# Grouped-query attention over a cache: K transposed as 4-byte words, and most of wo loaded behind V

## The chip, the cores and the metric

The kernel runs on one core of a Trainium2 chip. The metric is the device time in microseconds of one execution. Before the change the median of 11 runs is 196.08 us (195.16 to 197.15).

In the text PE is TensorE (matmuls and transposes), DVE is VectorE, ACT is ScalarE, POOL is GpSimd, and SP is the engine whose queue issues all DMA transfers here. SBUF is the on-chip memory, PSUM the memory into which PE writes.

## The reference

The kernel computes one attention block with keys and values from a cache, for 8 batches of 4 query tokens, all in bf16:

```python
B, Sq, D = 8, 4, 512
Hq, Hkv, Sk, Dh = 32, 8, 2048, 128
q = (x @ wq).reshape(B, Sq, Hq, Dh).transpose(0, 2, 1, 3)
k = jnp.repeat(k_cache, Hq // Hkv, axis=1)
v = jnp.repeat(v_cache, Hq // Hkv, axis=1)
p = softmax(einsum("bhqd,bhkd->bhqk", q, k) * Dh ** -0.5)
o = einsum("bhqk,bhkd->bhqd", p, v)
return o.transpose(0, 2, 1, 3).reshape(B, Sq, Hq * Dh) @ wo
```

k_cache and v_cache are 32 MB each, wq and wo 4 MB each. So some 72 MB are read once, and each key meets only the 16 query rows (4 heads of 4 tokens) of its group.

## The kernel before, in words

**Tiles.** Work is cut into 32 units: a pair p of K/V heads (4 of them, outer) and a batch b (8, inner). A unit's K block is one tile `k_sb` of 128 partitions: partitions 0 to 63 hold the first head of the pair, 64 to 127 the second, and each partition holds 32 successive keys of 128 numbers, 8 KB. A "chunk" is the 128 keys with one index c of these 32. One transfer of 1 MB loads it (L87); V is laid out in the same way (L97). There are 7 K buffers and 6 V buffers.

**Steps.** A unit has two steps of 16 chunks each. The loop at the end of the listing runs over the steps, and the order in which Python calls the helpers is the order on each engine: it is written out by hand. In one turn it transposes for step + 7, scores for step + 6, and does the values of the step itself.

- `transpose_part` (L169) turns 8 chunks of K, one PE transpose each, into one PSUM tile `kp` (3 buffers). The tile is copied to SBUF as `kt` (6 buffers) by DVE, and every fourth time by ACT (L172, L174).
- `scores` (L185) runs 16 matmuls per step. The weights are a transposed chunk, 128 by 128; the moving operand is q of both heads, 32 columns. So each key is scored with the queries of both heads, and the exponentials (L191, ACT) read the half that belongs to its own head, written to `probs`. The other half of `probs` stays zero.
- `values` (L205) runs 16 matmuls per step, V chunks as weights and 32 columns of `probs` moving.
- `norms` (L219) sums `probs` with two matmuls of 512 columns, and DVE reduces and inverts (L227, L231). `finish` (L236) scales into `oT_all`.

**The projection.** For each p, `to_tokens` (L248) and `to_wo_rows` (L263) rearrange the 8 heads of the pair into the rows in which wo was loaded, and `project` (L272) runs 8 matmuls of 512 columns, one for each eighth r of wo's block p. For p 0 and 1 this stands behind steps 59 and 61. For p 2 and 3 it follows the last step, with `to_tokens(3)` and `to_wo_rows(3)` between the parts of p 2. At the end DVE and ACT each convert half of the output and SP stores it.

**Transfers.** SP issues x, wq, and then the list `loads`: K of unit u, V of unit u - 3, and at its end wo blocks 0 and 1 between the last V blocks, so V 29, wo 0, V 30, wo 1, V 31. `load_ready` issues from the list as far as buffers allow. Behind step 51, wo block 2, and block 3 in three parts, are issued (L104). The schedule keeps eight transfers in flight.

**Start.** wq is needed whole before q can be made: 128 matmuls of 32 columns (L149), after which ACT scales q into `qT_all` (L156). The K transposes come after them on PE.

Of the kernel before, what the change touches and what calls it, by code (L numbers as in the profile page):

```python
# [8 lines left out]
BF16 = mybir.dt.bfloat16  # L9
FP32 = mybir.dt.float32  # L10
# [4 lines left out]
def kernel(  # L15
# [9 lines left out]
    nc = tc.nc  # L25

    B, Sq, D = x.shape
    _, Hkv, Sk, Dh = k_cache.shape
    HqDh = wq.shape[1]
# [3 lines left out]
    R = D // 128  # L33
    G2 = Hkv // 2
    C = 2 * Sk // 128
    NQ = 2 * rep * Sq
    HC = C // 2
    HP = 2 * rep
    scale = float(Dh) ** -0.5
    NU = G2 * B  # L40
    NH = 2 * NU
# [4 lines left out]
    WR = HP  # L46
# [4 lines left out]
    assert Dh == 128 and C == 32 and NQ == 32 and G2 == 4  # L51

    const = ctx.enter_context(tc.tile_pool(name="const", bufs=1))
    kpool = ctx.enter_context(tc.tile_pool(name="kpool", bufs=KB))
    vpool = ctx.enter_context(tc.tile_pool(name="vpool", bufs=VB))
    ktpool = ctx.enter_context(tc.tile_pool(name="ktpool", bufs=6))
    small = ctx.enter_context(tc.tile_pool(name="small", bufs=2))
    psum_k = ctx.enter_context(tc.tile_pool(name="psum_k", bufs=3, space=bass.MemoryType.PSUM))
    psum_s = ctx.enter_context(tc.tile_pool(name="psum_s", bufs=2, space=bass.MemoryType.PSUM))
# [4 lines left out]
    order = ctx.enter_context(tc.manual_schedule())  # L64

    x_sb = const.tile([T, D], BF16, name="x_sb")
    wq_sb = const.tile([128, R, HqDh], BF16, name="wq_sb")
    xT_sb = const.tile([128, R, T], BF16, name="xT_sb")
    qT_all = const.tile([128, G2, B, HP, Sq], BF16, name="qT_all")
    oT_all = const.tile([128, Hq, B, Sq], BF16, name="oT_all")  # L70
    wo_sb = const.tile([128, G2, WR, D], BF16, name="wo_sb")
    out_sb = const.tile([T, D], BF16, name="out_sb")
    oP = [const.tile([128, WR, T], BF16, name=f"oP{p}") for p in range(G2)]
    ident = const.tile([128, 128], BF16, name="ident")
# [4 lines left out]
    ks = [None] * NU  # L79
# [22 lines left out]
    def load_wo(p, r0, n):  # L102
        rows = wo[p * HP * 128 : (p + 1) * HP * 128, :].rearrange("(q r) j -> q r j", r=WR)
        nc.sync.dma_start(wo_sb[:, p, r0 : r0 + n, :], rows[:, r0 : r0 + n, :])  # L104
# [3 lines left out]
    loads = []  # L108
    for u in range(NU + KA):
        if u < NU:  # L110
            loads.append(("k", u))
        if u >= KA - 1 and u - KA + 1 < NU:
            loads.append(("v", u - KA + 1))
        if u in (NU, NU + 1):
            loads.append(("wo", u - NU))
    loads.reverse()

    def load_ready(nk, nv):
# [12 lines left out]
    load_ready(0, 0)  # L131

    make_identity(nc, ident[:])
    nc.vector.memset(ones[:, :], 1.0)
    for t in probs:
        nc.vector.memset(t[:, :, :], 0.0)
# [7 lines left out]
    for p in range(G2):  # L144
        psq = psum_s.tile([128, HP, T], FP32, tag="s", name="psq")
        for h in range(HP):
            hh = p * HP + h
            for r in range(R):
                nc.tensor.matmul(  # L149
                    psq[:, h, :],  # L150
                    lhsT=wq_sb[:, r, hh * 128 : (hh + 1) * 128],
                    rhs=xT_sb[:, r, :],
                    start=(r == 0),
                    stop=(r == R - 1),
                )
        nc.scalar.mul(  # L156
            out=qT_all[:, p, :, :, :],
            in_=psq[:, :, :].rearrange("d h (b s) -> d b h s", b=B),
            mul=scale,
        )  # L160

    kt = {}

    def transpose_part(i, part):
        u, hf = divmod(i, 2)
        c0 = hf * HC + part * (HC // 2)
        kp = psum_k.tile([128, HC // 2, 128], BF16, tag="k", name="kp")
        for c in range(HC // 2):
            nc.tensor.transpose(kp[:, c, :], ks[u][:, c0 + c, :], ident[:, :])  # L169
        k_t = ktpool.tile([128, HC // 2, 128], BF16, tag="kt", name="kt")  # L170
        if part == 1 and hf == 1:
            nc.scalar.copy(out=k_t[:, :, :], in_=kp[:, :, :])  # L172
        else:
            nc.vector.tensor_copy(out=k_t[:, :, :], in_=kp[:, :, :])  # L174
        kt[(i, part)] = k_t

    def scores(i):
        u, hf = divmod(i, 2)
        p, b = units[u]
        pr = probs[u % len(probs)]  # L180
        s_ps = psum_s.tile([128, HC, NQ], FP32, tag="s", name="s_ps")
        q2 = qT_all[:, p, b, :, :].rearrange("d h s -> d (h s)")
        for c in range(HC):
            k_t = kt[(i, c // (HC // 2))]
            nc.tensor.matmul(  # L185
                s_ps[:, c, :], lhsT=k_t[:, c % (HC // 2), :], rhs=q2, start=True, stop=True
            )
        for g in range(2):
            rows = slice(g * 64, (g + 1) * 64)
            cols = slice(g * NQ // 2, (g + 1) * NQ // 2)  # L190
            nc.scalar.activation(  # L191
                out=pr[rows, hf * HC : (hf + 1) * HC, cols], in_=s_ps[rows, :, cols], func=EXP
            )
# [3 lines left out]
    def values(i):  # L197
        u, hf = divmod(i, 2)
        p, b = units[u]
        pr = probs[u % len(probs)]  # L200
        if hf == 0:
            o_ps[u] = psum_o.tile([128, NQ], FP32, tag="o", name="o_ps")
        for c in range(HC):
            cc = hf * HC + c
            nc.tensor.matmul(  # L205
                o_ps[u][:, :],
                lhsT=vs[u][:, cc, :],
                rhs=pr[:, cc, :],
                start=(cc == 0),
                stop=(cc == C - 1),  # L210
            )
# [3 lines left out]
    def norms(u):  # L215
        pr = probs[u % len(probs)]
        l_ps = psum_l.tile([128, LC, NQ], FP32, tag="l", name="l_ps")
        for c in range(0, C, LC):
            nc.tensor.matmul(  # L219
                l_ps[:, :, :],  # L220
                lhsT=ones[:, :],
                rhs=pr[:, c : c + LC, :],
                start=(c == 0),
                stop=(c + LC == C),
            )
        l_sb = small.tile([128, NQ], FP32, tag="l_sb", name="l_sb")
        nc.vector.tensor_reduce(  # L227
            out=l_sb[:, :], in_=l_ps[:, :, :].rearrange("d c q -> d q c"), axis=AX, op=ADD
        )
        r_sb = small.tile([128, NQ], FP32, tag="r_sb", name="r_sb")  # L230
        nc.vector.reciprocal(r_sb[:, :], l_sb[:, :])  # L231
        r_sbs[u] = r_sb

    def finish(u):
        p, b = units[u]
        nc.vector.tensor_tensor(  # L236
            out=oT_all[:, p * HP : (p + 1) * HP, b, :],
            in0=o_ps[u][:, :].rearrange("d (h s) -> d h s", h=HP),
            in1=r_sbs[u][:, :].rearrange("d (h s) -> d h s", h=HP),
            op=mybir.AluOpType.mult,  # L240
        )
# [18 lines left out]
    def to_wo_rows(p):  # L260
        perm = psum_l.tile([128, WR, T], BF16, tag="l", name="perm")
        for r in range(WR):
            nc.tensor.transpose(  # L263
                perm[:, r, :],
                nats[p][:, :, :].rearrange("t q r -> t r q")[:, r, :],
                ident[:T, :T],
            )
        nc.vector.tensor_copy(out=oP[p][:, :, :], in_=perm[:, :, :])

    def project(p, r0, n):  # L270
        for r in range(r0, r0 + n):
            nc.tensor.matmul(  # L272
                out_ps[:, :],
                lhsT=oP[p][:, r, :],
                rhs=wo_sb[:, p, r, :],
                start=(p == 0 and r == 0),
                stop=(p == G2 - 1 and r == WR - 1),
            )

    for step in range(-L - 1, NH):  # L280
        i, j = step + L + 1, step + L
        if i < NH:
            transpose_part(i, 0)
        if 0 <= j < NH:
            scores(j)
        if i < NH:
            transpose_part(i, 1)
        u, hf = divmod(step, 2)
        if step >= 0:
            p, b = units[u]  # L290
            if hf == 1:
                norms(u)
            values(step)
            if hf == 1:
                finish(u)
            elif p > 0 and b == 1:
                to_tokens(p - 1)
            elif p > 0 and b == 2:
                to_wo_rows(p - 1)
        load_ready(min((i + 1) // 2, NU), max((step + 1) // 2, 0))  # L300
        if step == NH - 1 - 2 * VB:
            assert not loads
            load_wo(2, 0, WR)
            load_wo(3, 0, 4)
            load_wo(3, 4, 2)
            load_wo(3, 6, 2)
        if step == NH - 5:
            out_ps = psum_s.tile([T, D], FP32, tag="s", name="out_ps")
            project(0, 0, WR)
        elif step == NH - 3:  # L310
            project(1, 0, WR)

    to_tokens(3)
    project(2, 0, 4)
    to_wo_rows(3)
    project(2, 4, 4)
    project(3, 0, 4)
    project(3, 4, 2)
    project(3, 6, 2)
# [33 lines left out]
```

## Time and profile before

One profiled execution took 196.83 us. The page counts a span of 195.1 us from the first to the last instruction; 1.73 us lie around it.

| What | Value |
|---|---|
| Median of 11 runs | 196.08 us |
| Profiled execution, its span | 196.83 us, 195.1 us |
| PE busy | 150.3 us, 77% |
| DVE busy | 107.7 us, 55% |
| ACT busy | 84.0 us, 43% |
| DMA | 76.03 MB, 390 GB/s on average |
| K transposes, L169 | 1024, 222 ns each |
| Scores, L185 | 1024, 177 ns each |
| Copies of kt on DVE, on ACT | 96 of 688 ns, 32 of 1012 ns |

How to read it: matmuls run in a pipeline, so the 222 ns of one transpose is its latency; how far apart two of them start is what counts, and the timeline tells that. "busy tenths" gives for each engine 40 equal slices of the span, here 4.88 us each, with the busy share in tenths. PEclk is the share of its full clock that TensorE was granted. The chain that ended last goes back from the last instruction and names at each step what released it. In the timeline a line gives the start, the length, the engine and line of the source, output and inputs, and in brackets how long the engine sat idle before and what ended that.

### The profile page before, as it was taken

Reading aid. Unit: us, or ns where it says so; the run is one execution under the profiler, and the core shown is the slowest. Engines: PE = TensorE matmul, PEld = TensorE weight load, DVE = VectorE, ACT = ScalarE, POOL = GpSimd, SP = SyncE. Lnnn points to the kernel's source line nnn. Section 1 sums busy time; section 2 is a strip of 40 time slices with the busy share of each in tenths; the row PEclk is TensorE's granted clock in tenths of the full one; section 3 lists DMA queues with packets and bytes.
Section 4 is the critical chain, followed back from the end, with each engine's and each line's share of the span. In section 5 each row is a group of like instructions: output and inputs, shape, how many; then the busy total and the mean of one; then the engine's idle time right before and its main releaser. Section 6 shows DMA issues by size and latency. Waiting matters only on the chain.

```text
span 195.1 us, 7361 instructions
## 1 busy us (share of the span) xinstructions
PE 150.3 (77%) x3364; PEld 130.7 (67%) x3364; DVE 107.7 (55%) x211; ACT 84.0 (43%) x166; POOL 0.7 (0%) x6
## 2 busy tenths in 40 slices
PE   1029777999998876987877899599888899884973
PEld 0029767888887865877777788488777888752341
DVE  6002554677776764666666676466666676652040
ACT  2003676655554554555555545426655544530000
POOL 1000000000000000000000000000000000000000
PEclk9999999999999999999999999969999999998599
DMA  6999999999999999999999999999999999999610
GB/s 222 430 386 427 420 420 422 420 417 420 415 422 418 417 415 423 422 417 415 420 425 412 422 420 422 415 422 417 418 413 425 420 417 417 420 415 417 263 40 7
DMA packets 10351, 76.03 MB, mean 390 GB/s; under 512 B 1168, under 2 KB 1232, under 8 KB 1616
## 3 DMA queue, kind: packets, MB, share of 16 engines
q1 hardware_dynamic: 10320, 75.57, 93.5%
q8 instruction: 26, 0.43, 0.9%
q14 instruction: 5, 0.04, 0.1%
HBM read 75.53 MB, written 0.03 MB: 387 GB/s over the span
## 4 chain that ended last, share of the span: by engine, by line
DMA 80%; PE 12%; ACT 3%; DVE 2%; issue 1%; SPq 0%; DVEq 0%
DMA k_sb<-in_k_cache_dram 52%; DMA wo_sb<-in_wo_dram 11%; DMA v_sb<-in_v_cache_dram 10%; DMA wq_sb<-in_wq_dram 6%; PE out_ps L272 4%; PE kp L169 2%; ACT kt L172 2%; PE psq L149 2%; PE s_ps L185 2%; DVE kt L174 1%; ACT probs L191 1%; PE l_ps L219 1%; PE o_ps L205 0%; DVE l_sb L227 0%; PE nat L248 0%
## 5 line engine op out<-in xcount | busy, mean ns | idle before, releaser
L174 DVE COPY kt<-kp 128x1024 bf16<-128x1024 bf16 x96 | 65.7, 688 | 60.9 <-PE kp L169 60.9
L169 PE MATMUL kp<-ident,k_sb 128*128 128x128 bf16 x1024 | 78.6, 222 | 17.5 <-DMA k_sb<-in_k_cache_dram 17.4
L191 ACT ACTIVATE probs<-s_ps 64x256 bf16<-64x256 f32 x128 | 48.4, 378 | 73.7 <-PE s_ps L185 72.9
L169 PEld LDWEIGHTS <-k_sb 128*128 128x128 bf16 x1024 | 59.6, 98 | 19.9 <-DMA k_sb<-in_k_cache_dram 19.7
L185 PE MATMUL s_ps<-qT_all,kt 128*128 128x32 bf16 x1024 | 38.2, 177 | 6.0 <-ACT kt L172 4.7
L205 PEld LDWEIGHTS <-v_sb 128*128 128x128 bf16 x1024 | 33.9, 96 | 12.9 <-DMA v_sb<-in_v_cache_dram 3.4
L185 PEld LDWEIGHTS <-kt 128*128 128x128 bf16 x1024 | 33.4, 96 | 7.8 <-ACT kt L172 5.8
L205 PE MATMUL o_ps<-probs,v_sb 128*128 128x32 bf16 x1024 | 36.0, 177 | 2.8 <-DMA v_sb<-in_v_cache_dram 2.5
L172 ACT COPY kt<-kp 128x1024 bf16<-128x1024 bf16 x32 | 32.4, 1012 | 0.8
L227 DVE TENSOR_REDUCE l_sb<-l_ps 128x32 f32<-128x512 f32 x32 | 21.8, 682 | 10.8 <-PE l_ps L219 10.7
L219 PE MATMUL l_ps<-probs,ones 128*128 128x512 bf16 x64 | 19.9, 394 | 0.0
L231 DVE RECIPROCAL r_sb<-l_sb 128x32 f32<-128x32 f32 x32 | 11.3, 353 | 1.1
L149 PE MATMUL psq<-xT_sb,wq_sb 128*128 128x32 bf16 x128 | 3.6, 188 | 9.5 <-DMA wq_sb<-in_wq_dram 9.5
L272 PE MATMUL out_ps<-wo_sb,oP 128*32 128x512 bf16 x32 | 9.3, 441 | 1.1 <-DMA wo_sb<-in_wo_dram 1.1
L149 PEld LDWEIGHTS <-wq_sb 128*128 128x128 bf16 x128 | 3.5, 104 | 9.7 <-DMA wq_sb<-in_wq_dram 9.7
L321 ACT CAST out_sb<-out_ps 32x256 bf16<-32x256 f32 x1 | 0.4, 362 | 19.4 <-DVE out_sb L320 19.4
L236 DVE TENSOR_TENSOR oT_all<-o_ps,r_sb 128x32 bf16<-128x32 f32 x32 | 6.1, 192 | 3.3
L156 ACT ACTIVATE qT_all<-psq 128x256 bf16<-128x256 f32 x4 | 1.5, 385 | 14.0 <-PE psq L149 14.0
L272 PEld LDWEIGHTS <-oP 128*32 128x32 bf16 x32 | 3.2, 106 | 5.0 <-issue 2.7
L219 PEld LDWEIGHTS <-ones 128*128 128x128 bf16 x64 | 5.0, 100 | 0.1
L254 DVE COPY nat_sb<-nat 32x1024 bf16<-32x1024 bf16 x4 | 2.7, 678 | 2.6 <-PE nat L248 2.6
L248 PE MATMUL nat<-ident,oT_all 128*32 128x128 bf16 x32 | 2.5, 220 | 1.0 <-DVE oT_all L236 1.0
(17 smaller groups left out, 14.3 us busy)
## 6 DMA issues: line engine op xcount, KB each, us to landing
k_sb<-in_k_cache_dram SPq DMA_DIRECT2D x32, 1024.0 KB, 19.8
v_sb<-in_v_cache_dram SPq DMA_DIRECT2D x32, 1024.0 KB, 19.8
wq_sb<-in_wq_dram SPq DMA_DIRECT2D x1, 4096.0 KB, 12.4
wo_sb<-in_wo_dram SPq DMA_DIRECT2D x3, 1024.0 KB, 21.4
wo_sb<-in_wo_dram SPq DMA_DIRECT2D x1, 512.0 KB, 20.1
wo_sb<-in_wo_dram SPq DMA_DIRECT2D x2, 256.0 KB, 17.4
x_sb<-in_x_dram SPq DMA_DIRECT2D x1, 32.0 KB, 1.7
out_dram<-out_sb SPq DMA_DIRECT2D x1, 32.0 KB, 1.5
```

What stands on the lines that cost most here:

```text
L149: nc.tensor.matmul(psq[:, h, :], lhsT=wq_sb[:, r, hh * 128 : (hh + 1) * 128], rhs=xT_sb[:, r, :], start=(r == 0), stop=(r == R - 1),)
L169: nc.tensor.transpose(kp[:, c, :], ks[u][:, c0 + c, :], ident[:, :])
L172: nc.scalar.copy(out=k_t[:, :, :], in_=kp[:, :, :])
L174: nc.vector.tensor_copy(out=k_t[:, :, :], in_=kp[:, :, :])
L185: nc.tensor.matmul(s_ps[:, c, :], lhsT=k_t[:, c % (HC // 2), :], rhs=q2, start=True, stop=True)
L191: nc.scalar.activation(out=pr[rows, hf * HC : (hf + 1) * HC, cols], in_=s_ps[rows, :, cols], func=EXP)
L205: nc.tensor.matmul(o_ps[u][:, :], lhsT=vs[u][:, cc, :], rhs=pr[:, cc, :], start=(cc == 0), stop=(cc == C - 1),)
L219: nc.tensor.matmul(l_ps[:, :, :], lhsT=ones[:, :], rhs=pr[:, c : c + LC, :], start=(c == 0), stop=(c + LC == C),)
L227: nc.vector.tensor_reduce(out=l_sb[:, :], in_=l_ps[:, :, :].rearrange("d c q -> d q c"), axis=AX, op=ADD)
L231: nc.vector.reciprocal(r_sb[:, :], l_sb[:, :])
L236: nc.vector.tensor_tensor(out=oT_all[:, p * HP : (p + 1) * HP, b, :], in0=o_ps[u][:, :].rearrange("d (h s) -> d h s", h=HP), in1=r_sbs[u][ ...
L272: nc.tensor.matmul(out_ps[:, :], lhsT=oP[p][:, r, :], rhs=wo_sb[:, p, r, :], start=(p == 0 and r == 0), stop=(p == G2 - 1 and r == WR - 1),)
```

## The change

**K as 4-byte words.** `ks[u]` is read as 4-byte numbers. 128 such words are two neighbouring chunks of 128 bf16 numbers. One transpose with a 4-byte identity (`ident4`) thus handles two chunks, and 4 transposes fill a `kp` tile of the same size as before. Row k of the result holds word k: rows 0 to 63 are the pairs of numbers of the first chunk, rows 64 to 127 those of the second, and in each word the even number stands beside the odd one. The copy to `kt` reads and writes the same bits as bf16.

**Scores by even and odd rows.** With weights `k_t[:, j, :, e]` (every second number of a row) a matmul sees the even (e = 0) or odd (e = 1) numbers of both chunks. The moving operand `q_bd` is block-diagonal: its upper 64 rows hold the even (or odd) rows of q in the first 32 columns, its lower 64 rows hold them in the other 32, and the rest is zero. Two matmuls of 64 columns, added up in PSUM, give the scores of two chunks. The number of score matmuls stays 1024.

**q_bd** is made at the start: `pick` selects every second column of the identity, twice, so that 8 matmuls of 256 columns give the even and odd rows of q on both halves of the partitions, and 8 copies (4 on DVE, 4 on ACT) place them.

**wo** no longer has a buffer of its own but takes that of wq (`wpool`). Block 0 is loaded as before; block 1 goes behind V 31, ahead of blocks 2 and 3, and its projection moves behind the last step.

```diff
-    wq_sb = const.tile([128, R, HqDh], BF16, name="wq_sb")
+    wq_sb = wpool.tile([128, R, HqDh], BF16, tag="w", name="wq_sb")
...
+    q_bd = const.tile([128, G2, 2, B, 2, NQ], BF16, name="q_bd")
+    pick = const.tile([128, 2, 2, Dh // 2], BF16, name="pick")
+    ident4 = const.tile([128, 128], FP32, name="ident4")
...
-        if u in (NU, NU + 1):
-            loads.append(("wo", u - NU))
+        if u == NU:
+            loads.append(("wo", 0))
...
+    make_identity(nc, ident4[:])
+    for e in range(2):
+        for g in range(2):
+            nc.vector.tensor_copy(
+                out=pick[:, e, g, :], in_=ident[:, :].rearrange("d (k e) -> d e k", e=2)[:, e, :]
+            )
+    nc.vector.memset(q_bd[:, :, :, :, :, :], 0.0)
...
+    for p in range(G2):
+        pse = psum_s.tile([128, 2, B, NQ], FP32, tag="s", name="pse")
+        for e in range(2):
+            nc.tensor.matmul(
+                pse[:, e, :, :],
+                lhsT=pick[:, e, :, :],
+                rhs=qT_all[:, p, :, :, :].rearrange("d b h s -> d (b h s)"),
+                start=True,
+                stop=True,
+            )
+        for g in range(2):
+            rows = slice(g * 64, (g + 1) * 64)
+            (nc.scalar.copy if g else nc.vector.tensor_copy)(
+                out=q_bd[rows, p, :, :, g, :], in_=pse[rows, :, :, :]
+            )
+
+    wo_sb = wpool.tile([128, G2, WR, D], BF16, tag="w", name="wo_sb")
...
-        kp = psum_k.tile([128, HC // 2, 128], BF16, tag="k", name="kp")
-        for c in range(HC // 2):
-            nc.tensor.transpose(kp[:, c, :], ks[u][:, c0 + c, :], ident[:, :])
-        k_t = ktpool.tile([128, HC // 2, 128], BF16, tag="kt", name="kt")
+        kp = psum_k.tile([128, HC // 4, 128], FP32, tag="k", name="kp")
+        k4 = ks[u][:, :, :].rearrange("s c d -> s (c d)").bitcast(FP32)
+        for j in range(HC // 4):
+            w = (c0 // 2 + j) * 128
+            nc.tensor.transpose(kp[:, j, :], k4[:, w : w + 128], ident4[:, :])
+        kp2 = kp[:, :, :].rearrange("k j s -> k (j s)").bitcast(BF16)
+        k_t = ktpool.tile([128, HC // 4, 128, 2], BF16, tag="kt", name="kt")
+        kt2 = k_t[:, :, :, :].rearrange("k j s e -> k (j s e)")
...
-        for c in range(HC):
-            k_t = kt[(i, c // (HC // 2))]
-            nc.tensor.matmul(
-                s_ps[:, c, :], lhsT=k_t[:, c % (HC // 2), :], rhs=q2, start=True, stop=True
-            )
+        for j in range(HC // 2):
+            k_t = kt[(i, j // (HC // 4))]
+            for e in range(2):
+                nc.tensor.matmul(
+                    s_ps[:, 2 * j : 2 * j + 2, :],
+                    lhsT=k_t[:, j % (HC // 4), :, e],
+                    rhs=q_bd[:, p, e, b, :, :],
+                    start=(e == 0),
+                    stop=(e == 1),
+                )
...
+            load_wo(1, 0, WR)
             load_wo(2, 0, WR)
...
-        elif step == NH - 3:
-            project(1, 0, WR)
 
     to_tokens(3)
-    project(2, 0, 4)
+    project(1, 0, 4)
     to_wo_rows(3)
-    project(2, 4, 4)
+    project(1, 4, 4)
+    project(2, 0, WR)
     project(3, 0, 4)
```

## The prediction

> **What bounds the kernel now.** I read the page's slices first, then its DMA queues, then the chain that ended last, and last the timeline of one block and of the tail.
>
> From the page, the slices and the queues:
>
> ```profile
> PE   1029777999998876987877899599888899884973
> PEclk9999999999999999999999999969999999998599
> DMA  6999999999999999999999999999999999999610
> ...
> q1 hardware_dynamic: 10320, 75.57, 93.5%
> q8 instruction: 26, 0.43, 0.9%
> ```
>
> DMA is full from slice 1 to slice 36 and ends some 10 us before the span does; PE is never full for long. The second queue is small but matters below: 26 fetches of instructions. The chain in order of time says the same:
>
> ```profile
> 95.70 19.82 DMA k_sb<-in_k_cache_dram
> 115.53 0.02 issue
> 115.55 21.36 DMA k_sb<-in_k_cache_dram
> ...
> 159.20 21.38 DMA wo_sb<-in_wo_dram
> 180.59 0.04 issue
> 180.63 3.57 PE out_ps L272 x8
> 184.20 0.54 PE o_ps L205 x16
> ```
>
> Each 1 MB load takes 19.8 us because eight are in flight. By the semaphore increments in the trace they land every 2.48 us, so a K and a V block cost 4.96 us. Four landings come some 1.5 us late (two show here as 21.4 instead of 19.8). After 181 us the loads are thin, and three things follow one another: block 1 of wo lands at 180.6, its projection runs at the half clock, and only then come the last values. One block in the timeline, from one wait for K to the next:
>
> ```profile
> 64.44 0.62 PE L169 MATMUL kp<-ident,k_sb 128*128 128x128 bf16 x8 [0.49 <-DMA k_sb<-in_k_cache_dram]
> 64.89 0.56 PE L185 MATMUL s_ps<-qT_all,kt 128*128 128x32 bf16 x16
> ...
> 67.93 0.56 PE L205 MATMUL o_ps<-probs,v_sb 128*128 128x32 bf16 x16
> ...
> 69.39 0.62 PE L169 MATMUL kp<-ident,k_sb 128*128 128x128 bf16 x8 [0.90 <-DMA k_sb<-in_k_cache_dram]
> ```
>
> PE's work ends at 68.49, so a block is 4.05 us of PE in 4.96 us. PE has 0.9 us to spare.
>
> **The skill.** (1) The Trainium skill, "TensorE: Matmul & The Clock Gate", Terms, says that the transpose mode of weight loads and matmuls is four times faster for FP32: I read it as one pass. No row of before shows a 4-byte transpose. (2) The same page, "Weight-path perf modes — Fast Weight Load (FWL) and DoubleRow", says the fast load needs 128 weights and a type other than FP32, and may be strided. The trace agrees that loads are cheap: loads of 128 columns with 32-column matmuls start 25 ns apart (L185), and 26.7 ns apart at the half clock (L149). (3) "Runtime: NRT & Kernel Launch", Instruction fetch mechanics, has instructions come in 16 KiB blocks of 256 and calls the cost mostly hidden. The size agrees (26 packets of 16,384 bytes, 1.02 to 1.15 us each; 6,730 PE instructions / 256 = 26.3). The hiding doesn't: fetches 1, 9, 17 and 25, at 19.4, 70.1, 121.3 and 174.3, each come some 3 us before one of the late landings. (4) The first page, Part 1, has the clock judged in free-running windows of 3.4 us; the trace's two clock drops last 3.4 and 6.8 us.
>
> **The change part by part.**
> *Transposes.* Per block 32 of 2 bytes (55.8 ns apart, 1.79 us) become 16 of 4 bytes. Lower bound: the load overlaps as now, 56 ns, 0.90 us. Middle: no fast load (four times 26.7 ns at half clock is 53 ns at full) and no overlap, 109 ns, 1.74 us. Upper: four passes of 53 ns, 216 ns, 3.46 us. I take 56 to 109, by the skill's one pass.
> *Scores.* Still 32 per block, now 64 columns wide with weights two elements apart. Half of a 128-column transpose is 29 ns; that gives 0.93 us against 0.80. The upper bound is L263, whose weights are eight elements apart: 62 ns, 1.98 us. I take 29: a step of 4 bytes is nearer to none.
> *Sum for PE.* 4.05 - 1.79 - 0.80 = 1.46 for the rest. With 0.90 + 0.93 it is 3.29 us, with 1.74 + 0.93 it is 4.13, both under 4.96. So the main part stays bound by DMA and the transposes' saving is hidden.
> *Evacuation.* The copies still move 128x1024 2-byte elements (688 ns DVE, 1012 ns ACT); exponentials keep their shape. Nothing.
> *Set-up.* A clear of q_bd (four times the 485 ns of one clear of probs, 1.9 us), four small copies, another identity: all before wq lands at 13.53, hidden. After it come 8 matmuls of 256 columns and 8 copies of 64x512, about 0.6 us each (between ACT's 378 ns for 256 and 1012 for 1024), with two PSUM buffers in rotation. PE's first transpose comes some 2.3 us later than its 17.17, and the first scores wait behind these copies on DVE and ACT. DMA is not touched: eight loads are queued, and seven K buffers let the eighth K load go out at 24.8. PE's 0.9 us per block takes it back in three blocks; without that cover it would cost 2.3 us.
> *Instruction fetches.* PE's stream shrinks from 6,730 to 4,818 rows (to 5,330 if a 4-byte transpose is still a load and a matmul): 18 to 20 fetches. The increments of the last wo load show what a fetch costs: six of 16 DMA engines finish by 182.3, six at 186.2 to 186.5, two at 187.9 and 188.06, steps of about 1.5 us. Fetches go round eight engines; 26 hit two of them four times, 18 to 24 hit none more than three times. The last landing moves from 188.06 to about 186.5. Upper bound of the gain 1.55 us, lower nothing.
> *wo.* On SP's queue wo block 1 moves from before the last V to behind it, ahead of wo 2 and 3; bytes are the same. The wait on wq's readers (wo takes its buffer) ended by 17.2. The last V takes wo 1's landing, 180.59 - 1.55 = 179.05, wo 1 the V's, 181.5; wo 2 about 184.0, wo 3 in parts 185.2 to 186.5.
> *Tail.* At full clock the last values lead to the token transposes 2.4 us later (178.15 to 180.56 for a like pair): 181.5. Then 8 transposes 0.45, 4 projections at 216 ns 0.86, the permutes 0.5, 4 projections 0.86 (184.2), 8 with wo 2 (186.0), 4 (186.8), and 4 more behind the last landing, 187.7. Before it was 191.84. With the half clock throughout (427 ns) the same ends at 193.3; warm again by 185 to 188.3, at 189 to 191. V 30 now lands at 176.55, so PE's idle time ahead of it shrinks from 2.0 to 0.45 us, but idle times of 1 us before and after the last values keep the half clock possible, and PE has less work throughout. I take 188.8, 3.0 us earlier.
> *Total.* The profiled execution took 196.83 us for a span of 195.1, 1.73 around it, and was in a slow tail, 0.75 above the median. 196.83 - 3.0 = 193.8.
>
> **Rivals.**
> *Transposes in four passes, or loads that don't overlap them (slower).* Place: L199's line of after. PE becomes the bound: 19.5 of start + 32 blocks + 1.9 (projection 0) + 10.8 (9.1 from the end of the last values in before, and 8 more projections) + 1.73. At 216 ns a block is 1.46 + 0.93 + 3.46 = 5.85, the total 221 us; with a separate load, 269 ns, 248. It decides from 5.07 us a block, 168 ns a transpose. For: the type excludes the fast load. Against: the skill's one pass.
> *Strided score weights cost as much as L263's, and transposes 109 ns (slower).* 1.46 + 1.98 + 1.74 = 5.18 a block: 200 us, up to 207 with the transposes at 120 and PE's gaps. With 56 ns it is 4.34 and hidden.
> *The body is hidden, and the tail gives nothing (the same).* Fetches hit as before or the half clock holds: 24 projections now stand behind the last V instead of 16, and 8 more at 427 ns are 3.4 us, which eats the V's 2.5 us: 196.
>
> **How the numbers follow.** The first case has 0.61, with a range of its own of 192.0 to 196.3; the tail that gives nothing 0.10; strided weights 0.16; four passes 0.13. From no change a measurement of this kernel tells about 0.3%, 0.6 us. Faster: 0.57 of the first case and 0.02 of the second, 0.59. Same: 0.09. Slower: 0.32. The time is the first case's, 193.8. The range runs from 191.9 (3 in 100 below) to 207, which takes in the strided weights and leaves out the four passes and 3 in 100 beside them.
>
> **What would show it.** Transposes: 56 to 109 ns apart, and PE waiting for K loads by 1 us or more per block. Scores: 29 ns apart. Queue 8: 18 to 20 fetches, and three late landings instead of four. The last V before wo 1, last landing near 186.5, and clock 0.9 or more after 181 if the tail went well. Wrong: a DMA row with gaps, K loads held back by buffers, and a full PE row; then the transposes or the scores carry the blame by their own spacing.

## The result and the profile after

The changed kernel takes 194.58 us in the median of 13 runs (193.32 to 194.78), against 196.04 us before (48 runs, 195.16 to 197.17). The ratio is 0.9906, with a 95% interval of 0.9882 to 0.9929: about 1.5 us faster. The forecast was 193.8 us. The profiled execution took 194.62 us for a span of 192.8.

From the page after, the slices and the instruction queue:

```profile
PE   0017778899999999998878899888885999989593
PEclk9999999999999999999999999999997899999888
DMA  6989999999999999999999999999999999999820
...
q8 instruction: 22, 0.36, 0.8%
```

DMA is full up to slice 36 as before, but for an 8 in slice 2, so the main part is still bound by it. PE is fuller than before, not emptier: 81% busy against 77%. The instruction queue has 22 fetches instead of 26. The groups of the two operations that were changed (busy us, mean ns, then idle time before):

```profile
L199 PE MATMUL kp<-ident,k_sb 128*128 128x128 f32 x512 | 80.3, 282 | 10.0 <-DMA k_sb<-in_k_cache_dram 9.8
...
L217 PE MATMUL s_ps<-q_bd,kt 128*128 128x64 bf16 x1024 | 44.0, 194 | 6.9 <-ACT kt L204 6.0
```

In the page before, the line of the transposes was:

```profile
L169 PE MATMUL kp<-ident,k_sb 128*128 128x128 bf16 x1024 | 78.6, 222 | 17.5 <-DMA k_sb<-in_k_cache_dram 17.4
```

PE's wait for K loads in the transposes fell from 17.4 us to 9.8 us in total. One block in the timeline after, up to the first transposes of the next; no wait for K falls into it, so its length is PE's own:

```profile
65.10 0.63 PE L199 MATMUL kp<-ident,k_sb 128*128 128x128 f32 x4
65.57 0.63 PE L217 MATMUL s_ps<-q_bd,kt 128*128 128x64 bf16 x16
...
68.09 0.41 PE L217 MATMUL s_ps<-q_bd,kt 128*128 128x64 bf16 x8 [0.32 <-ACT kt L204]
...
69.65 0.64 PE L199 MATMUL kp<-ident,k_sb 128*128 128x128 f32 x4
```

Four transposes take 0.47 us of PE (65.10 to 65.57): in the instruction records they follow one another after 109 ns, the second after 144. The eight 2-byte ones that they replace took 0.45 us (64.44 to 64.89 in the block before). So halving the number of transposes saved PE no time. The scores start 29 ns apart.

The chain after, its second half:

```profile
125.69 21.08 DMA k_sb<-in_k_cache_dram
...
160.04 19.28 DMA v_sb<-in_v_cache_dram
179.32 0.05 issue
179.37 0.56 PE o_ps L241 x16
...
181.84 1.04 PE nat L284 x8
182.88 1.71 PE out_ps L308 x4
184.58 0.61 PE perm L299 x8
185.19 4.43 PE out_ps L308 x20
```

The wait for wo and the projection that stood between the last loads and the last values are gone. The last V lands at 179.32 instead of 183.06, the last part of wo at 186.79 instead of 188.06 (both from the semaphore increments). The last projection ends at 189.62 instead of 191.84.

The landings stand some 2.5 us apart, and three come about 1.2 us later than that: those at 22.14, 83.21 and 144.29 us, 2.3 to 3.9 us behind the starts of fetches 1, 9 and 17 (19.3, 80.9 and 140.4). Before there were four, behind fetches 1, 9, 17 and 25. With fewer instructions fetches 9 and 17 come later, and there is no 25th.

Granted clock in the tail after, in stretches of 2 us (PE, PEld, DVE, ACT and POOL busy; then the clock, the DMA share, GB/s):

```profile
178.00:180.00 2.00, 0.91 (x30) 0.69 (x26) 1.16 (x3) 0.00 (x0) 0.00 (x0) 1.00 0.99 408
180.00:182.00 2.00, 0.92 (x20) 0.70 (x19) 1.24 (x3) 0.00 (x0) 0.00 (x0) 0.89 0.93 365
182.00:184.00 2.00, 2.00 (x12) 1.12 (x10) 0.68 (x1) 0.00 (x0) 0.00 (x0) 0.50 0.56 227
184.00:186.00 2.00, 2.00 (x15) 0.99 (x14) 0.29 (x1) 0.00 (x0) 0.00 (x0) 0.76 0.41 162
```

The clock is halved for about 3.4 us, from 181.5 to 185, just when the projections begin. The runs form two groups: nine lie at 194.47 to 194.78 with a mean clock of 0.979 to 0.982, four at 193.32 to 193.42 with 0.990 to 1.000. The kernel has two times, 1.2 us apart, and no run took the 193.8 us of the forecast.

### The profile page after: what moved, and what is told of

The parts are those of the page before. It is cut to its first block, busy times and chain, and to the rows that moved or that the text cites. A ratio compares the mean times of both kernels' runs of the same rounds, so it can differ in the third digit from the quotient of the medians.

```text
span 192.8 us, 6394 instructions
## 1 busy us (share of the span) xinstructions
PE 156.2 (81%) x2860; PEld 136.2 (71%) x2860; DVE 112.1 (58%) x220; ACT 86.3 (45%) x170; POOL 1.1 (1%) x8
## 4 chain that ended last, share of the span: by engine, by line
DMA 84%; PE 10%; SPq 1%; ACT 1%; DVE 1%; issue 1%; DVEq 0%
DMA k_sb<-in_k_cache_dram 74%; DMA v_sb<-in_v_cache_dram 10%; PE out_ps L308 3%; PE kp L199 2%; PE s_ps L217 1%; PE o_ps L241 1%; PE l_ps L255 1%; PE nat L284 1%; SPq L92 1%; ACT kt L204 1%; DVE l_sb L263 0%; PE perm L299 0%; DVE out_sb L356 0%; SPq L112 0%; ACT probs L227 0%
## 5 line engine op out<-in xcount | busy, mean ns | idle before, releaser
L199 PE MATMUL kp<-ident,k_sb 128*128 128x128 f32 x512 | 80.3, 282 | 10.0 <-DMA k_sb<-in_k_cache_dram 9.8
L199 PEld LDWEIGHTS kp<-ident,k_sb 128*128 128x128 f32 x512 | 54.5, 142 | 11.4 <-issue 10.5
L217 PE MATMUL s_ps<-q_bd,kt 128*128 128x64 bf16 x1024 | 44.0, 194 | 6.9 <-ACT kt L204 6.0
L217 PEld LDWEIGHTS <-kt 128*128 128x128 bf16 x1024 | 39.9, 98 | 10.1 <-ACT kt L204 7.7
L241 PEld LDWEIGHTS <-v_sb 128*128 128x128 bf16 x1024 | 34.8, 96 | 10.2 <-DMA v_sb<-in_v_cache_dram 1.9
L241 PE MATMUL o_ps<-probs,v_sb 128*128 128x32 bf16 x1024 | 35.4, 177 | 1.3 <-DMA v_sb<-in_v_cache_dram 1.3
L255 PE MATMUL l_ps<-probs,ones 128*128 128x512 bf16 x64 | 19.5, 387 | 0.0
L185 DVE CAST q_bd<-pse 64x512 bf16<-64x512 f32 x4 | 2.6, 678 | 10.6 <-PE pse L176 10.6
L308 PE MATMUL out_ps<-wo_sb,oP 128*32 128x512 bf16 x32 | 8.3, 412 | 0.0
L255 PEld LDWEIGHTS <-ones 128*128 128x128 bf16 x64 | 6.1, 99 | 0.4
L152 PE MATMUL xtp<-ident,x_sb 32*128 32x32 bf16 x4 | 0.5, 190 | 6.8 <-DVE xT_sb L155 4.3
```

The source lines that it names most:

```text
L199: nc.tensor.transpose(kp[:, j, :], k4[:, w : w + 128], ident4[:, :])
L217: nc.tensor.matmul(s_ps[:, 2 * j : 2 * j + 2, :], lhsT=k_t[:, j % (HC // 4), :, e], rhs=q_bd[:, p, e, b, :, :], start=(e == 0), stop=(e == 1),
L241: nc.tensor.matmul(o_ps[u][:, :], lhsT=vs[u][:, cc, :], rhs=pr[:, cc, :], start=(cc == 0), stop=(cc == C - 1),)
L255: nc.tensor.matmul(l_ps[:, :, :], lhsT=ones[:, :], rhs=pr[:, c : c + LC, :], start=(c == 0), stop=(c + LC == C),)
L308: nc.tensor.matmul(out_ps[:, :], lhsT=oP[p][:, r, :], rhs=wo_sb[:, p, r, :], start=(p == 0 and r == 0), stop=(p == G2 - 1 and r == WR - 1),)
```

## The experiments

The theory is the prediction's: the body is hidden behind DMA, and the gain has two sources. PE's shorter instruction stream takes a fetch from the DMA engine that ends last, so one of the four late landings drops out. And the last V no longer waits behind a block of wo. The rivals: the order of wo alone makes the gain; or PE's own work, not its fetches, does.

All results in one table. "Fetches" and "last landing" (of wo's last part) are of the profiled execution, times are medians and extremes of the timed runs.

| Kernel | Fetches | Last landing, us | Median, us | Runs, us |
|---|---|---|---|---|
| before | 26 | 188.06 | 196.04 | 195.16 to 197.17 |
| changed | 22 | 186.79 | 194.58 | 193.32 to 194.78 |
| e1, order of wo alone | 26 | 188.25 | 196.15 | 194.58 to 197.71 |
| e2, words alone | 22 | 186.83 | 194.14 | 194.06 to 194.31 |
| e3, changed, 490 idle pairs at the start | 26 | 189.35 | 198.35 | 197.77 to 198.51 |
| e4, changed, 122 longer pairs at the start | 23 | 186.78 | 194.02 | 193.23 to 194.79 |
| e5, changed, values cut to a quarter | 17 | 185.54 | 192.93 | 191.74 to 194.27 |
| e6, changed, values cut to a half | 18 | 186.75 | 193.92 | 193.25 to 195.46 |
| e9, changed, 490 idle pairs spread | 26 | 188.27 | 196.31 | 194.37 to 196.88 |
| e10, changed, longer pairs spread | 23 | 186.80 | 193.27 | 193.23 to 193.36 |
| e7, changed, tail kept warm | 22 | 187.16 | 193.46 | 193.24 to 193.71 |
| e8, before, tail kept warm | 26 | 188.29 | 195.46 | 195.17 to 196.66 |
| e11, order of wo, tail kept warm | 26 | 188.02 | 194.55 | 194.47 to 194.79 |
| e12, before, values cut to a half | 22 | 187.16 | 194.72 | 194.03 to 195.74 |

### One part alone

**e1, the order of wo alone.**

```diff
--- before
-        if u in (NU, NU + 1):
-            loads.append(("wo", u - NU))
+        if u == NU:
+            loads.append(("wo", 0))
...
+            load_wo(1, 0, WR)
             load_wo(2, 0, WR)
...
-        elif step == NH - 3:
-            project(1, 0, WR)
...
-    project(2, 0, 4)
+    project(1, 0, 4)
     to_wo_rows(3)
-    project(2, 4, 4)
+    project(1, 4, 4)
+    project(2, 0, WR)
```

> The kernel before with the move of wo block 1 alone (transposes and scores as before). Fetch theory (the DMA stream ends when the DMA engine with the most instruction fetches does): 26 fetches as before, four late landings, last landing 188.1 us, the last V near 180.6 instead of 183.1, but 24 projections behind it, 8 of them more at up to 427 ns: 196.0 us, between 195.2 and 197. Rival (the order of wo alone makes the gain): 194.6 us.

Measured: 196.15 us, ratio to before 0.998 (0.9951 to 1.0009). The order of wo alone makes no difference that can be told, as expected. The tail in its timeline:

```profile
180.85 0.61 PE L205 MATMUL o_ps<-probs,v_sb 128*128 128x32 bf16 x16 [0.61 <-DMA v_sb<-in_v_cache_dram]
...
183.64 0.62 PE L248 MATMUL nat<-ident,oT_all 128*32 128x128 bf16 x8 [1.07 <-DVE oT_all L236]
...
185.65 4.49 PE L272 MATMUL out_ps<-wo_sb,oP 128*32 128x512 bf16 x20
```

In before the last values started here:

```profile
184.13 0.61 PE L205 MATMUL o_ps<-probs,v_sb 128*128 128x32 bf16 x16
```

They start 3.3 us earlier now, but 20 projections stand at the end where 12 did. This profiled execution took 195.14 us; the runs go from 194.58 to 197.71, wider than before's on both sides.

**e2, the words alone.**

```diff
--- changed
-        if u == NU:
-            loads.append(("wo", 0))
+        if u in (NU, NU + 1):
+            loads.append(("wo", u - NU))
...
-            load_wo(1, 0, WR)
...
+        elif step == NH - 3:
+            project(1, 0, WR)
```

(and the order of the projections at the end as before)

> The changed kernel with wo block 1 back ahead of the last V and its projection behind step 61 (words and score form kept). Fetch theory: 22 fetches, three late landings, last landing 186.8 us, tail as before but 1.3 us earlier: 194.8 us, between 194 and 195.8. Rival (the order of wo alone makes the gain): 196.0 us.

Measured: 194.14 us, ratio 0.9894 (0.9858 to 0.9929). By medians the words alone carry the whole of the gain, and a little more. But the clock in the tail differs: nine of the changed kernel's 13 runs are in its slower group, while the five runs of e2 lie within 0.25 us. At the full clock the order of wo does add something (e11 and e7, below). The page of e2 has no dip of the clock in the tail:

```profile
PEclk9999999999999999999999999999999999999999
```

### Is it the instruction fetches?

**e3, more instructions at the start.** Pairs of a small weight load and matmul, whose results nobody reads, bring PE's stream back to the length of before.

```diff
--- changed
+    dum = psum_l.tile([32, 16], FP32, tag="l", name="dum")
+
+    def pad(n):
+        for _ in range(n):
+            nc.tensor.matmul(
+                dum[:, :], lhsT=ident[:, :32], rhs=ident[:, :16], start=True, stop=True
+            )
+
+    pad(250)
     for r in range(R):
         xtp = psum_o.tile([128, T], BF16, tag="o", name="xtp")
...
+    pad(240)
     for p in range(G2):
         psq = psum_s.tile([128, HP, T], FP32, tag="s", name="psq")
```

> The changed kernel with 490 idle pairs of weight load and matmul (32 columns of weights, 16 columns moving) put on PE while it waits for wq, results unused. Fetch theory: 26 fetches again, a fourth late landing near 174 us, last landing 188.1 us, 195.8 us. Rival (fetches don't matter, PE's smaller work does): 194.6 us as the changed kernel, last landing 186.8 us.

Measured: 198.35 us, ratio 1.0101 (1.007 to 1.0132), 2.5 us more than was expected. The timeline of PE at its start shows why:

```profile
1.35 6.12 PE L154 MATMUL dum<-ident 128*32 128x16 bf16 x223 [1.35 <-POOL ident masks.py:199]
10.61 0.87 PE L154 MATMUL dum<-ident 128*32 128x16 bf16 x27 [3.14 <-issue]
...
17.36 3.56 PE L154 MATMUL dum<-ident 128*32 128x16 bf16 x128 [2.53 <-issue]
23.29 0.55 PE L154 MATMUL dum<-ident 128*32 128x16 bf16 x15 [2.36 <-issue]
...
29.75 0.43 PE L171 MATMUL psq<-xT_sb,wq_sb 128*128 128x32 bf16 x10 [2.80 <-issue]
```

PE stopped four times for 2.4 to 3.1 us without any semaphore to wait for, once after 128 pairs, that is 256 instructions: I read it as waiting for its next block of instructions, whose fetch shares the DMA engines with the loads. The times fit: the first four fetches start at 8.2, 15.1, 20.9 and 27.4 us, and each time PE goes on 2.3 to 2.4 us later (10.61, 17.36, 23.29, 29.75). Work that stood at 13.5 us now stood at 24, K buffers came free late, and the DMA row fell to 348 and 353 GB/s in slices 10 and 12. So this run mixes two things and decides nothing on the count of fetches. It was replaced by e9.

**e4, its control.** 122 pairs of 128 columns in the same places.

```diff
--- changed
+    dum = psum_l.tile([128, 128], FP32, tag="l", name="dum")
+    (as in e3, with lhsT=ident[:, :128], rhs=ident[:, :128], pad(62) and pad(60))
```

> Control for the padded kernel: about the same PE time in the wait for wq in 122 pairs of 128 columns, so 23 fetches at most. Fetch theory: three late landings, last landing 186.8 us, 194.6 us. If the padding hurts by its PE time or by a later start, this one is as slow as the one with 490 pairs: 195.8 us.

Measured: 194.02 us, 186.78 us for the last landing, ratio 0.9886 (0.9847 to 0.9926). PE's time in the wait for wq costs nothing, although the first K transpose moves from 19.75 to 21.15 us.

**e9, more instructions, spread.** The 490 pairs again, but slowly enough for the fetches.

```diff
--- changed
+    dum = psum_l.tile([32, 32], FP32, tag="l", name="dum")
+    for _ in range(106):
+        nc.tensor.matmul(dum[:, :], lhsT=ident[:, :32], rhs=ident[:, :32], start=True, stop=True)
...
             o_ps[u] = psum_o.tile([128, NQ], FP32, tag="o", name="o_ps")
+            for _ in range(12):
+                nc.tensor.matmul(
+                    o_ps[u][:32, :16], lhsT=ident[:, :32], rhs=ident[:, :16], start=True, stop=True
+                )
```

> The changed kernel with the same 490 idle pairs, now 106 at the start and 12 ahead of the values of each unit, some 0.32 us of PE per unit out of the 0.4 us that are free. Fetch theory: 26 fetches, the fourth late landing is back, last landing 188.1 us, 195.6 us. Rival: 194.6 us, last landing 186.8 us.

**e10, its control.** The same PE time per unit in fewer instructions.

```diff
--- changed
-            o_ps[u] = psum_o.tile([128, NQ], FP32, tag="o", name="o_ps")
+            o_big = psum_o.tile([128, 160], FP32, tag="o", name="o_ps")
+            o_ps[u] = o_big[:, :NQ]
+            for _ in range(5):
+                nc.tensor.matmul(
+                    o_big[:, :],
+                    lhsT=ident[:, :],
+                    rhs=qT_all[:, 0, 0:5, :, :].rearrange("d b h s -> d (b h s)"),
+                    start=True,
+                    stop=True,
+                )
```

> Control: 5 idle pairs of 160 columns ahead of the values of each unit, the same 0.33 us of PE per unit in 23 fetches. Fetch theory: three late landings, last landing 186.8 us, 194.6 us or less. If PE's lack of free time is what hurts the padded kernel, this one is as slow: 195.6 us.

Measured: e9 196.31 us, ratio 0.9992 (0.9959 to 1.0025), 0.7 us more than was expected: the gain is gone. e10 193.27 us, ratio 0.9858 (0.9829 to 0.9888): the gain is there. The queues of the two pages, e9 and then e10:

```profile
q8 instruction: 26, 0.43, 0.9%
```

```profile
q8 instruction: 23, 0.38, 0.8%
```

Both keep DMA full up to slice 36 as the changed kernel does. e9's last loads land 1.47 us later (188.27 against 186.80), and a late landing stands at 178.3 as in the kernel before, 2.3 us after fetch 25. PE's time is nearly the same: the idle pairs take 0.39 us per unit in e9 and 0.35 in e10. Nor did PE hold up the loads in e9, since the DMA engines that end first do so at the same time (181.8 us, in the excerpt below). So it is the number of instructions that delays the landing.

The medians differ by more than that, 3.0 us. e9 has two groups of runs, as the changed kernel has: five at 194.37 to 194.83 and nine at 195.93 to 196.88. Between the lower group and e10, whose six runs lie at 193.23 to 193.36, it is some 1.4 us, the delay of the landing. The rest goes with the group, and probably with the clock in the tail: e10's idle columns also fill PE's gaps there.

**e5 and e6, fewer instructions than the changed kernel.** Part of the value matmuls is left out in the first 30 units; loads and the tail stay.

```diff
--- changed
         for c in range(HC):
             cc = hf * HC + c
+            if u < NU - 2 and cc % 4:      (e6: cc % 2)
+                continue
...
-                stop=(cc == C - 1),
+                stop=(cc == (C - 1 if u >= NU - 2 else C - 4)),      (e6: C - 2)
```

> The changed kernel with three of four value matmuls left out in the first 30 units (their V blocks are still loaded): PE's stream falls to 16 fetches. Fetch theory: no DMA engine is hit more than twice, two late landings, last landing 185.5 us, time 192.1 to 193.6 us depending on the clock in the tail. Rival (what counts is the number of instructions or PE's free time, not the hits on one engine): the gain is in proportion, or nothing.

> The changed kernel with every second value matmul left out in the first 30 units: 18 fetches. Fetch theory: three hits on the worst engine as with 22, last landing 186.8 us, no gain over the changed kernel: 193.3 to 194.7 us. Rival (gain in proportion to the instructions left out): last landing 186.1 us or less, half way to the kernel with 16 fetches or more.

Measured: the last landing is 186.75 us with 18 fetches, as with 22, and 185.54 us in e5. e5 has a 17th fetch, but it comes at 185.0 us, when the loads are all but over. Medians are 193.92 us (e6) and 192.93 us (e5). Both have two groups of runs as well; the lower ones are 193.25 to 193.40 for e6, as the changed kernel's four runs at 193.32 to 193.42, and 191.74 to 192.03 for e5. Cutting 960 instructions gave the landing nothing, cutting 1,440 gave it 1.25 us: the gain comes in steps, as eight engines taken in turn would have it. e5's late landings are two, at 22.6 and 101.0 us, behind fetches 1 and 9. The increments of wo's last part, in us, tell the same (an excerpt of the trace, one number for each of the 16 DMA engines):

```
before   181.8 182.0 182.1 182.1 182.3 182.3 183.6 183.8 186.2 186.3 186.3 186.3 186.5 186.5 187.9 188.1
changed  181.8 181.9 182.0 182.1 182.2 182.4 183.5 183.9 184.9 185.0 186.4 186.4 186.5 186.7 186.7 186.8
e6       182.0 182.1 182.2 182.3 182.4 182.7 183.2 183.7 184.9 185.0 185.0 185.1 185.2 185.2 186.4 186.8
e5       181.8 181.9 182.0 182.1 182.2 182.4 183.5 183.9 184.9 185.0 185.0 185.2 185.2 185.3 185.3 185.5
e9       181.8 181.8 182.0 182.1 182.2 182.4 183.2 183.9 186.4 186.6 186.6 186.6 186.6 186.7 188.0 188.3
e10      181.6 181.7 181.8 181.9 182.1 182.5 183.1 183.7 184.8 186.4 186.5 186.5 186.7 186.7 186.7 186.8
```

The last eight numbers of a line stand near 185, 186.5 or 188 us. Read as engines with two, three or four fetches, they give the number of fetches each time: two engines with 4 and six with 3 in before (26 = 2 x 4 + 6 x 3), six with 3 and two with 2 in the changed kernel (22), two with 3 and six with 2 in e6 (18), eight with 2 in e5 (16 before the loads end), the same in e9 as in before (26), seven with 3 and one with 2 in e10 (23). Which engine a fetch used is not in the trace; this is worked out from the landings.

**e12, the kernel before with 22 fetches and no 4-byte word.** The edit of e6 on the kernel before.

> The kernel before with every second value matmul left out in the first 30 units (V is still loaded), no 4-byte word in it: 22 fetches as the changed kernel. Fetch theory: three late landings, last landing 186.8 us, 1.3 us less than before: 194.0 to 195.8 us, median 194.8 us. Rival (the transposes or the scores themselves make the gain): 196.1 us, last landing 188.1 us.

Measured: 194.72 us, ratio 0.9936 (0.9911 to 0.9961), last landing 187.16 us. Its queue:

```profile
q8 instruction: 22, 0.36, 0.8%
```

A shorter PE stream alone, with 2-byte transposes and the old order of wo, brings the kernel before to within 0.2 us of the changed one. PE is also freer there, but DMA is full as before, so that the time freed should be hidden. The last landing of e12 and of e7 is 0.4 us later than in the other kernels with 22 fetches; why is not shown.

### The clock in the tail

**e7, the changed kernel with idle matmuls in the gaps.**

```diff
--- changed
+    def warm(n):
+        w_ps = psum_k.tile([128, 256], FP32, tag="k", name="w_ps")
+        for _ in range(n):
+            nc.tensor.matmul(
+                w_ps[:, :],
+                lhsT=ident[:, :],
+                rhs=qT_all[:, 0, :, :, :].rearrange("d b h s -> d (b h s)"),
+                start=True,
+                stop=True,
+            )
+
...
             project(0, 0, WR)
+            warm(2)
+        elif step == NH - 3:
+            warm(8)
 
+    warm(8)
     to_tokens(3)
```

> The changed kernel with idle matmuls of 256 columns in PE's gaps of the tail: 2 behind projection 0, 8 ahead of the last values, 8 ahead of the last token transposes. Clock theory (the changed kernel's two groups of times, 193.4 and 194.6, are one tail at the full clock and at the half clock): all runs 193.2 to 193.5 us, last landing 186.8 us as before. Rival (the two groups come from the transfers): still two groups, the last landing differing between them.

**e8, the kernel before with idle matmuls.** `warm(18)` behind `project(0, 0, WR)` and `warm(8)` ahead of `project(1, 0, WR)`.

> The kernel before with idle matmuls of 256 columns in its gaps: 18 behind projection 0 and 8 ahead of projection 1. Clock theory: its spread from 195.2 to 197.2 us closes at its lower end, 195.2 us, last landing 188.1 us. Then of the changed kernel's gain 1.9 us remain at the full clock. Rival (the spread has another cause): median 196.1 us.

**e11, e1 with idle matmuls.** `warm(18)` behind `project(0, 0, WR)`, `warm(8)` in step 61 and `warm(8)` ahead of `to_tokens(3)`.

> The move of wo block 1 alone, with idle matmuls in the gaps (18 behind projection 0, 8 ahead of the last values, 8 ahead of the last token transposes). Clock theory: the move is worth 0.5 to 0.9 us once the clock holds, and was hidden by the half clock: 194.5 us, last landing 188.1 us. Rival (the eight projections more behind the last V always eat the gain): 195.2 us.

Measured: e7 193.46 us (193.24 to 193.71), ratio 0.986 (0.9833 to 0.9887). The upper group of times is gone in its five runs. e8 195.46 us, ratio 0.9968 (0.9951 to 0.9985), 0.3 us above what was expected, with one of 20 runs at 196.66. e11 194.55 us, ratio 0.9919 (0.9892 to 0.9946). Clock rows of e7, e8 and e11:

```profile
PEclk9999999999999999999999999999999799999999
```

```profile
PEclk9999999999999999999999999957999999999999
```

```profile
PEclk9999999999999999999999999969999999999998
```

The dips in the body are still there; those from slice 37 on are gone, but for the 8 in e11's last slice, which lies behind its last matmul. What changed is seen at the last values and the token transposes, first in the changed kernel, then in e7:

```profile
179.37 0.56 PE L241 MATMUL o_ps<-probs,v_sb 128*128 128x32 bf16 x16 [1.09 <-DMA v_sb<-in_v_cache_dram]
...
181.84 1.04 PE L284 MATMUL nat<-ident,oT_all 128*32 128x128 bf16 x8 [1.08 <-DVE oT_all L272]
```

```profile
179.72 0.56 PE L241 MATMUL o_ps<-probs,v_sb 128*128 128x32 bf16 x16 [0.20 <-DMA v_sb<-in_v_cache_dram]
...
182.19 0.62 PE L284 MATMUL nat<-ident,oT_all 128*32 128x128 bf16 x8 [0.19 <-DVE oT_all L272]
```

With these two idle times of 1.1 us filled the clock stayed up. With the clock held the parts can be set side by side: before 195.46 (e8), order of wo -0.91 (e11 against e8), words -1.32 (e2, whose page shows the full clock, against e8), both together -2.0 (e7 against e8). The two parts add up to 2.2, so 0.2 us is lost where they meet. By medians the changed kernel reached 1.5 us, as nine of its 13 runs are in the slower group. Probably it is the move of wo that brings the half clock there: e2, which has eight projections between the last two V blocks, shows none of it. But the kernel before has them too, and its clock fell, behind an idle time of 2.0 us ahead of V 30; so the rule is not known. e7 is the fastest complete version of this study but for e10 (193.27 us), whose idle work was put in as a control and keeps the clock up too.

## Why the prediction was right

**Body hidden, right.** The transposes came out at the middle value of the prediction, 109 ns. It was a sum of a load of 53 ns and a matmul of 56 that don't overlap. No run takes the two apart, and the prediction gave no measurement for the four times by which its plain load is slower, so the spacing is shown and its parts are not. The scores came out at the value taken, 29 ns: no cost of the strided weights is seen. A block was put at 3.29 to 4.13 us of PE and takes 4.55, more than both: the sum left out the 144 ns in each group of four transposes (0.14 us a block), and the 0.32 us for which half the scores wait for ACT's copy. So PE was nearer to being the bound than forecast, with 0.4 us to spare out of 4.96, and it waited for K loads 13 times and 9.8 us in total, not by 1 us or more per block. Neither of the slower rivals came true: transposes stayed under the 168 ns from which they decide. The prediction read the Trainium skill ("TensorE: Matmul & The Clock Gate", Terms: the transpose mode is four times faster for FP32) as one pass; 109 ns agrees with that, and not with the 216 put down for four passes.

**Set-up, right.** The first transpose starts at 19.75 us; 19.5 was forecast. e4 moved it to 21.15 and lost nothing.

**Fetches, right in kind, wrong in count.** 18 to 20 were forecast, 22 came. The 4,818 to 5,330 rows that the prediction counted were too few: the profile's 2,860 matmuls and 2,860 loads make 5,720, and 5,720 / 256 is 22.3. The change itself gives that number: from 6,730 go two instructions for each of 512 transposes, and 16 come in for `q_bd`. It did no harm, since with eight engines in turn 17 to 24 fetches all hit the worst engine three times. The last landing moved by 1.27 us; 1.55 was forecast. e12, with 22 fetches and no 4-byte word, shows most of the gain.

**wo and the tail, right in order, too hopeful in size.** Forecast and measured: last V at 179.05 and 179.32, wo 1 at 181.5 and 181.82, last landing 186.5 and 186.79, last projection 188.8 and 189.62. The term that was mis-sized is the tail: 3.0 us were taken, 2.2 were measured between the two profiled executions, with the half clock on the projections for 3.4 us. The prediction had named this, and took a value between its two ends; the half clock turned out to be the more frequent case. From the median of before, 196.08, the forecast of 193.8 was a gain of 2.3 us, and 1.5 came. That 193.8 lies close to the result is in part luck: it stands between the kernel's two times, 193.4 and 194.6.

**The rival that came nearest** is that the tail gives nothing. For the order of wo by itself it is what e1 measured. With the clock held the order of wo gave 0.9 us (e11). The rival did not decide, because the fetches gave their part regardless.

## What to carry to other kernels

When a stream of loads fills DMA, count the instruction fetches as part of it. Here the stream ended with the DMA engine that was hit most often: a shorter PE program was worth 1.3 us where PE itself had time to spare (e12), and the last landing moved in steps of 1.2 to 1.5 us, one for some eight fetches. Look at PE's gaps ahead of its last, dense piece of work: in the changed kernel idle times of 1.1 us came with a half clock on the projections, and 18 idle matmuls in the gaps took the median from 194.58 to 193.46 us. And an operation that does twice as much per instruction should be costed by how far apart its instructions start, not by their number.

## What the runs showed of the hardware that was not expected

- In e3 PE ran through 128 short pairs in 3.56 us and then stopped for 2.36 us without a semaphore to wait for, while DMA was full; it went on 2.4 us after a fetch of instructions had started. That it waited for this fetch is a reading.
- By the landings, fetches of PE's instructions hit only eight of the 16 DMA engines; six engines end at about 182 us in every kernel here but e3, whose loads were held up, with 17 fetches as with 26. Each fetch took 1.02 to 1.15 us in the kernel before and put its engine back by some 1.5 us.
- 4-byte transposes of 128x128 start 109 ns apart, the second of a group 144 ns after the first, against 56 ns for 2 bytes: twice the bytes in twice the time.
